# Top-k attention with an MLP behind it: the MLP's input formed in columns from reciprocals that go through HBM, the mean taken out of the weights, and the rows turned back later

## The chip, the cores and the metric

The kernel runs on one core of one Trainium2 chip, one launch. The metric is the device time of that core in microseconds (us). The kernel before took 1569.79 us, the median of three runs (1568.69 to 1570.04).

Engines are named as in the profile: PE (TensorE matmuls; PEld its weight loads), DVE (VectorE), ACT (ScalarE), POOL (GpSimd), SP (SyncE, which here issues DMAs). Each works through its own list of instructions in order and waits for the others at semaphores.

## The reference

Two parts follow each other. The attention has 8 batches, 8 heads, 576 rows and head size 64; each row keeps its 32 largest scores:

```python
scores = scale * np.matmul(q, k.transpose(0, 1, 3, 2))
kth = np.partition(scores, -top_k, axis=-1)[..., -top_k:-top_k + 1]
scores = np.where(scores >= kth, scores, -1000000000.0)
attn = np.exp(scores - np.max(scores, axis=-1, keepdims=True))
attn = attn / (np.sum(attn, axis=-1, keepdims=True) + 1e-09)
attn_out = np.matmul(attn, v)          # (B, H, S, D), then x = (B, S, H*D)
```

Then an MLP with a normalisation in front and a residual, with 512 columns and a hidden width of 2048:

```python
mu = np.mean(x, axis=-1, keepdims=True)
var = np.mean((x - mu) ** 2, axis=-1, keepdims=True)
xn = (x - mu) / np.sqrt(var + 1e-06) * g_ln
return x + np.maximum(xn @ w_ch1, 0.0) @ w_ch2
```

The two weight matrices arrive as 64-bit numbers.

## The kernel before, in words

**Units, groups, blocks.** The attention is cut into 160 *units*: 128 queries of a pair of heads (`hp`, four pairs in a batch), or, for the last 64 queries of a batch, the *rest* of both heads in one unit. One to three units with the same keys are a *group* (80 of them). When all four head pairs of a batch have given the values of 256 queries, these make a *block* of two 128-row tiles for the MLP; the rests of four batches make a block too. There are 18 blocks.

**Steps.** The main loop runs over n. In step n, unit n goes through the search for its 32 largest on DVE (`halve`, then four rounds of `select`), unit n+2 through its scores on PE, unit n-1 through its mask (ACT, then POOL L535) and exponentials (ACT L543, `weigh`, which also gives the row sums `den`), and an older unit is turned, by PE or by DVE and a way through HBM (`move`, `pt<-turned`), so that a group's `values` can be multiplied on PE a *lag* of two to four steps after its last unit. What an engine does in which order is fixed by this program order.

**Filling.** The MLP's matmuls stand in a list, `todo`. Eight times in a step `fill` takes from it as much as a planner gives (`slot` in step n spreads what is left evenly up to the next block that joins, at `give`), unless the first item may not yet run. Ages counted in such ticks also set when late work (`Later`) is issued.

**From values to the MLP, before.** `values` leaves the product for a group in PSUM, transposed: 128 partitions are two heads' 64 columns, the free axis is the queries. `take_values` (L687, ACT) copies it to oT. `place` turns each 128 queries back with a PE transpose (`xo`, L714), and `put` (L691, ACT) copies the two heads' halves to the rows x, each scaled by its row's reciprocal sum, which is a number per partition there. Rests are gathered by POOL (L705) from two batches, and their sums by small DMAs (`keep_den`, L659), for `place_rest` (L721). A step after the last head pair `stats` takes mean and variance on DVE (L742, L743) and the row's mean is taken off x, on DVE for block 0 (L745), on POOL later (L748, L751). Six ticks later `turn_x` turns the rows into xT (PE L778, ACT L781). Then 64 matmuls with w1 (`hidden`, L819), ReLU (L842), and the projection with w2: plainly (L858) for two blocks, by a scheme with seven products instead of eight (L979, with sums on POOL) for the others. `finish` multiplies by rstd and adds the mean (ACT L797), adds x (POOL L790) and stores.

**Weights.** In steps 0 to 20 the 32 pieces of w1 and w2 (128x512 numbers each) are fetched and made into float32: `split` on ACT and POOL (L164 to L169; for w1, the sign is also multiplied by the gain g_ln on POOL, L171), `shift` on DVE (L177), `join` on POOL (L183, L185). A hidden or projection matmul may be issued one step after its piece is `ready`.

Of the kernel before, what the change touches and what calls it, by code (L numbers as in the profile page):

```python
# [29 lines left out]
def compute(  # L30
# [42 lines left out]
    otpool = pool("ot", 1)  # L73
    restpool = pool("ot_rest", 1)
# [3 lines left out]
    xpool = pool("x", 4)  # L78
    rpool = pool("r", 2)
# [3 lines left out]
    xtpool = pool("xt", 1)  # L83
# [29 lines left out]
    columns = const([P, J + NC], "columns")  # L113
    half, gcol = columns[:, 0:J], columns[:, J : J + NC]
    nc.gpsimd.memset(half[:], -0.5)
    w1 = const([P, NC, DFF], "w1")
# [6 lines left out]
    class Piece:  # L123
# [22 lines left out]
        def fetch(self):  # L146
            self.raw = xpool.tile([P, DM, 2], U32, tag="x", name="raw")
            nc.sync.dma_start(self.raw[:].rearrange("p n w -> p (n w)"), self.src)

        def split(self):  # L150
            i = self.i
            high = self.raw[:, :, 1].bitcast(FP32)
            if i < 3 * NC:
                self.size = hpool.tile([P, DM], U32, tag="h", name="size")[:]
                self.low = wt_rows[:, i % 8]
                homes = ((opool, "o"), (opool, "o"), (rpool, "r"), (rpool, "r"), (xtpool, "xT"))
            else:
                self.size = wt_rows[:, 2 * i % 8].bitcast(U32)
                self.low = wt_rows[:, (2 * i + 1) % 8]
                homes = ((opool, "o"), (opool, "o"), (rpool, "r"))  # L160
# [9 lines left out]
            if self.i < NF:  # L170
                nc.gpsimd.tensor_scalar(  # L171
                    self.sign[:], self.sign[:], gcol[:, self.c : self.c + 1], 1.0,
                    ALU.mult, ALU.mult,
                )
# [6 lines left out]
        def join(self):  # L181
# [4 lines left out]
            ready[self.i] = now[0]  # L186
# [3 lines left out]
    ready = [None] * (2 * NF)  # L190
    pieces = [Piece(i) for i in range(2 * NF)]
# [3 lines left out]
    def load_gain():  # L195
        ps = turned()
        nc.tensor.transpose(ps[:, 0:NC], grow[:], ident[0:NC, 0:NC])
        nc.scalar.copy(gcol[:], ps[:, 0:NC])

# [337 lines left out]
    def weigh(u, t):  # L537
# [3 lines left out]
        col = 2 * u.qt + t  # L541
# [5 lines left out]
        if u.rest:  # L547
            den = g.den[:, 2 * J : 2 * J + 1]
        elif u.weighed == 2 and u is [x for x in g.units if not x.rest][-1]:
            whole = [qt for qt in g.qts if qt < J]  # L550
            den = g.den[:, 2 * whole[0] : 2 * whole[-1] + 2]
            g.sums = den
        else:
            return
        nc.scalar.activation(den, den, AF.Copy, bias=DEN_EPS)
# [94 lines left out]
    xs, xps, rs, oTr, dr = {}, {}, {}, {}, {}  # L650

    def keep_den(u):

        b, hp = u.job.b, u.job.hp
        if (b // 2) not in dr:
            dr[b // 2] = denpool.tile([P, H], FP32, tag="dr", name="dr")
        r0 = R * (b % 2)
        for h in range(2):
            nc.sync.dma_start(  # L659
                dr[b // 2][r0 : r0 + R, 2 * hp + h : 2 * hp + h + 1],  # L660
                u.group.den[h * R : (h + 1) * R, 2 * J : 2 * J + 1],
            )
# [21 lines left out]

    def take_values(g):
        g.oT = otpool.tile([P, GQ], FP32, tag="oT", name="oT")
        nc.scalar.copy(g.oT[:, 0 : g.nq], g.av[:, 0 : g.nq])  # L687

    def put(dst, ps, c0, den, d0):
        for h in range(2):  # L690
            nc.scalar.mul(  # L691
                dst[:, c0 + h * D : c0 + (h + 1) * D],
                ps[:, h * D : (h + 1) * D],
                den[:, d0 + h : d0 + h + 1],
            )

    def place(g):

        b, hp = g.job.b, g.job.hp
        for i, qt in enumerate(g.qts):  # L700
            if qt == J:
                if b % 2 == 0:
                    oTr[hp] = restpool.tile([P, P], FP32, tag=f"oTr{hp}", name="oTr")
                r0 = R * (b % 2)
                nc.gpsimd.tensor_copy(  # L705
                    oTr[hp][:, r0 : r0 + R], g.oT[:, i * P : i * P + R]
                )
                continue
            if (b, qt) not in xs:
                pair = xpool.tile([P, 2, DM], FP32, tag="x", name="x")  # L710
                for j in range(2):
                    xs[b, qt // 2 * 2 + j] = pair[:, j]
            ps = brief("xo")
            nc.tensor.transpose(ps[:, 0:P], g.oT[:, i * P : (i + 1) * P], ident[:])  # L714
            put(xs[b, qt], ps, hp * P, g.den, 2 * qt)

    def place_rest(b, hp):
        if hp == 0:
            rs[b // 2] = rpool.tile([P, DM], FP32, tag="r", name="r")[:]
        ps = brief("xo")  # L720
        nc.tensor.transpose(ps[:, 0:P], oTr[hp][:], ident[:])  # L721
        put(rs[b // 2], ps, hp * P, dr[b // 2], 2 * hp)

    class Block:
        def __init__(self, tiles, dsts):
# [4 lines left out]
            self.step = {}  # L732
# [3 lines left out]
        def stats(self, i):  # L736
# [5 lines left out]
            nc.vector.bn_stats(out=st[:], in_=x)  # L742
            nc.vector.bn_aggr(out=self.mv[:, i, :], in_=st[:])  # L743
            if now[0] <= gives_first:
                nc.vector.tensor_scalar_sub(x, x, self.mv[:, i, 0:1])  # L745
            else:
                less = brief_small.tile([P, 1], FP32, tag="less", name="less")
                nc.gpsimd.tensor_scalar(  # L748
                    less[:], self.mv[:, i, 0:1], -1.0, 0.0, ALU.mult, ALU.add
# [727 lines left out]
```

## Time and profile before

| | |
|---|---|
| median of three runs | 1569.79 us (1568.69 to 1570.04) |
| the profiled execution, its time | 1571.11 us |
| the profiled execution, its span | 1569.2 us |
| granted TensorE clock, mean | 0.975 |
| HBM traffic over the span | 155 GB/s |

The span runs from the first to the last instruction on the core; the time holds a little more around it. A row of groups reads: line, engine, operation, out<-in, shapes, count | busy us, mean ns of one | idle time of the engine just before them, and what ended it. A row of waits reads: engine and line that waited <- what it waited for: us in total, times, longest. A row in order of time reads: start us, length us, engine, line, operation, with the idle time before it in brackets. Durations of PE are those of overlapping, modelled instructions. Lines of DMA issues give the median time from issue to landing as their last number.

### The profile page before, as it was taken

Reading aid. Unit: us, or ns where it says so; the run is one execution under the profiler, and the core shown is the slowest. Engines: PE = TensorE matmul, PEld = TensorE weight load, DVE = VectorE, ACT = ScalarE, POOL = GpSimd, SP = SyncE. Lnnn points to the kernel's source line nnn. Section 1 sums busy time; section 2 is a strip of 40 time slices with the busy share of each in tenths; the row PEclk is TensorE's granted clock in tenths of the full one; section 3 lists DMA queues with packets and bytes.
Section 4 is the critical chain, followed back from the end, with each engine's and each line's share of the span. In section 5 each row is a group of like instructions: output and inputs, shape, how many; then the busy total and the mean of one; then the engine's idle time right before and its main releaser. Section 6 shows DMA issues by size and latency. Waiting matters only on the chain. (4 is left out here: it accounts for less than half of the span.)

```text
span 1569.2 us, 27215 instructions
## 1 busy us (share of the span) xinstructions
PE 1469.0 (94%) x8046; PEld 1108.0 (71%) x8046; DVE 1363.4 (87%) x3873; ACT 1083.8 (69%) x3081; POOL 981.2 (63%) x1318
## 2 busy tenths in 40 slices
PE   4568889999999999999999999999999998999997
PEld 3346446566787677778777777777777776788886
DVE  7997999899979998999988999999999999768000
ACT  6978887786777767767768676768676776555421
POOL 6968995747465565756566647474746475737524
PEclk9779989999999999999999999999999999999999
DMA  6623551466728865577754687657677557454511
GB/s 170 167 85 97 137 139 53 124 178 181 226 83 194 202 208 153 168 199 153 216 148 134 174 200 197 173 150 191 175 201 206 162 164 208 121 166 125 150 35 50
DMA packets 374774, 245.60 MB, mean 157 GB/s; under 512 B 255956, under 2 KB 343512, under 8 KB 374616
## 3 DMA queue, kind: packets, MB, share of 16 engines
q1 hardware_dynamic: 371048, 243.17, 57.6%
q8 instruction: 67, 1.10, 0.3%
q10 hardware_dynamic: 3568, 0.59, 0.3%
q14 instruction: 91, 0.75, 0.2%
HBM read 166.14 MB, written 77.53 MB: 155 GB/s over the span
## 5 line engine op out<-in xcount | busy, mean ns | idle before, releaser
L535 POOL TENSOR_TENSOR e<-e,sc 128x576 f32<-128x576 f32 x288 | 416.0, 1462 | 453.8 <-ACT e L532 392.9
L819 PE MATMUL hps<-xT,w 128*128 128x256 f32 x2304 | 542.2, 384 | 2.4 <-ACT xT L781 2.4
L819 PEld LDWEIGHTS hps<-xT,w 128*128 128x128 f32 x2304 | 423.0, 191 | 82.2 <-issue 27.2
L483 DVE MAX8 m<-hi 128x8 f32<-128x296 f32 (+1 forms) x1152 | 471.3, 444 | 1.2
L469 DVE MATCH_REPLACE8 hi<-m,hi 128x288 f32<-128x288 f32 (+1 forms) x864 | 377.0, 441 | 0.0
L979 PE MATMUL ops<-w,h 128*128 128x256 f32 x1280 | 304.8, 383 | 1.4 <-ACT o L944 1.4
L979 PEld LDWEIGHTS ops<-w,h 128*128 128x128 f32 x1280 | 233.6, 190 | 44.3 <-issue 13.5
L419 ACT COPY sc<-scps 128x288 f32<-128x288 f32 x576 | 188.5, 402 | 78.5 <-POOL e L535 56.2
L543 ACT ACTIVATE e<-e,m 128x576 f32<-128x576 f32 x288 | 225.1, 784 | 14.6 <-POOL e L535 12.5
L532 ACT ACTIVATE e<-sc,m 128x576 f32<-128x576 f32 x288 | 209.4, 769 | 0.0
L842 ACT ACTIVATE h<-hps 128x512 f32<-128x512 f32 x144 | 86.7, 602 | 114.1 <-PE hps L819 113.5
L577 DVE STREAM_TRANSPOSE sc<-e 128x1152 f32<-128x1152 f32 x87 | 118.8, 1366 | 52.5 <-ACT e L543 46.3
L669 PE MATMUL av<-pt,vb 128*64 128x256 f32 (+2 forms) x1280 | 148.8, 376 | 9.5 <-DMA pt<-turned 7.7
L462 DVE TENSOR_TENSOR lo<-sc 128x576 f32<-128x576 f32 (+1 forms) x160 | 136.1, 850 | 0.0
L461 DVE TENSOR_TENSOR hi<-sc 128x576 f32<-128x576 f32 (+1 forms) x160 | 130.0, 812 | 3.0 <-ACT sc L419 3.0
L669 PEld LDWEIGHTS av<-pt,vb 128*64 128x64 f32 x1280 | 81.6, 140 | 66.4 <-issue 17.1
L438 PE MATMUL scps<-kT,late_qT 64*128 64x288 f32 (+3 forms) x832 | 121.7, 410 | 0.2 <-ACT pt L618 0.2
L979 PE MATMUL ops<-wt,s 128*128 128x256 f32 x512 | 119.4, 383 | 0.0
L475 DVE MAX8 hi<-lo 128x8 f32<-128x288 f32 x288 | 117.5, 443 | 0.0
L438 PE MATMUL scps<-kT,qT 64*128 64x288 f32 x512 | 92.6, 460 | 23.5 <-DVE qT L366 8.0
L606 PE MATMUL tp<-ident,e 128*128 128x128 f32 x456 | 74.2, 290 | 39.9 <-ACT e L543 28.9
L979 PEld LDWEIGHTS ops<-wt,s 128*128 128x128 f32 x512 | 94.7, 190 | 17.3 <-issue 4.4
(111 smaller groups left out, 1793.5 us busy)
## 6 DMA issues: line engine op xcount, KB each, us to landing
turned<-sc SPq DMA_DIRECT2D x87, 576.0 KB, 4.2
pt<-turned SPq DMA_DIRECT2D x348, 144.0 KB, 3.2
w<-forms SPq DMA_DIRECT2D x128, 256.0 KB, 4.7
vb<-in_v_dram SPq DMA_DIRECT2D x80, 288.0 KB, 4.2
raw<-in_moe_w_ch_dram SPq DMA_DIRECT2D x32, 512.0 KB, 4.5
kT<-kept SPq DMA_DIRECT2D x48, 288.0 KB, 3.7
kept<-kT SPq DMA_DIRECT2D x32, 288.0 KB, 3.6
kqin<-in_k_dram SPq DMA_DIRECT2D x116, 72.0 KB, 2.6
```

The source lines that it names most:

```text
L419: nc.scalar.copy(u.sc[:, t, s * HALF : (s + 1) * HALF], u.made[s][t][:, 0:HALF])
L438: nc.tensor.matmul(ps[i * R : i * R + ql, o : o + width], qT[r, q0 : q0 + ql], kT[r, k0 : k0 + width], start=True, stop=True,)
L461: nc.vector.tensor_tensor(hi, a, b, ALU.max)
L462: nc.vector.tensor_tensor(lo, a, b, ALU.min)
L469: nc.vector.match_replace(x, m[:, t, :], x, LOWEST)
L483: nc.vector.max(m[:, t, :], u.hi[:, t, r0 : r0 + width])
L532: nc.scalar.activation(u.e[:, t], u.sc[:, t], AF.Relu, bias=u.edge[:, t : t + 1], scale=-STEEP)
L535: nc.gpsimd.tensor_tensor(u.e[:, t], u.e[:, t], u.sc[:, t], ALU.subtract)
L543: nc.scalar.activation(u.e[:, t], u.e[:, t], AF.Exp, bias=u.bias[:, t : t + 1], scale=-scale, accum_out=g.den[:, col : col + 1],)
L669: nc.tensor.matmul(av[h * D : (h + 1) * D, 0 : g.nq], vb[:, h * (J + 1) + c, :], heads_of(g, h, 0, g.nq // 32)[:, :, c], start=(c == 0), s ...
L819: nc.tensor.matmul(ps[0][:, side * N : (side + 1) * N], w1[:, c, f * P : (f + 1) * P], self.xT[:, c, 0:N], start=(c == 0), stop=(c == NC - 1),
L979: nc.tensor.matmul(bank[name][:, 0:Q], a(j), rhs, start=first and j == 0, stop=(j == G - 1), skip_group_check=not first,)
```

## The change

What the MLP takes is now formed without turning the values first. `take_values` copies the product straight into its place in xT (or rTs for rests). The reciprocals of a group's sums are taken in one DVE instruction, sent to HBM number by number (`keep_shares`), and read back spread over the 64 partitions of each head (`fetch_shares`); POOL multiplies xT by them in place (`place`). The mean is taken out of the weights: with W the gain-scaled w1, (x - mean(x)) @ W = x @ (W - column means of W), so a PE product with a matrix that holds -g/512 gives the column means on all partitions (`means`), and one DVE instruction for each of the 16 pieces forms W*g + mean in place (`centre`); the product with g on POOL goes. A piece of w1 is `ready` after that. The hidden matmuls start on xT at once; after the first 24 of them `turn_x` turns xT back to rows x, for statistics and the residual. `finish` no longer adds the mean.

The pools move too: x has three buffers for a row tile each, xT three, the rests' xT two, the shares one; the raw weights lie in those of xT. Before the second tile of a block is turned, `close` issues what is still waiting of the block before.

```diff
             nc.scalar.activation(self.sign[:], high, AF.Sign)
-            if self.i < NF:
-                nc.gpsimd.tensor_scalar(
-                    self.sign[:], self.sign[:], gcol[:, self.c : self.c + 1], 1.0,
-                    ALU.mult, ALU.mult,
-                )
...
+    def means(n):
+        nb = centred_parts[0]
+        if nb * NC >= NF or not all(map(done, joined[nb * NC : (nb + 1) * NC])):
+            return None
+        centred_parts[0] += 1
+        ps = product("mean")
+        for c in range(NC):
+            nc.tensor.matmul(
+                ps[:], gmean[:, c * P : (c + 1) * P], pieces[nb * NC + c].dst,
+                start=(c == 0), stop=(c == NC - 1),
+            )
+        return nb, ps
+
+    def centre(made, cs):
+        nb, ps = made
+        for c in cs:
+            x = pieces[nb * NC + c]
+            nc.vector.scalar_tensor_tensor(
+                x.dst, x.dst, gcol[:, c : c + 1], ps[:], ALU.mult, ALU.add
+            )
+            ready[x.i] = now[0]
...
+    def keep_shares(g):
+        nc.vector.reciprocal(g.sums, g.sums)
+        kept = g.kept = hbmpool.tile([2 * J + 1, P], FP32, tag="shares", name="shares")
+        n = g.sums.shape[1]
+        sends.add(lambda: nc.sync.dma_start(kept[0:n].rearrange("c p -> p c"), g.sums))
+
+    def fetch_shares(g):
+        t = g.shares = sharepool.tile([P, GQ], FP32, tag="shares", name="shares")
+        n = sum(qt < J for qt in g.qts)
         for h in range(2):
-            nc.sync.dma_start(
-                dr[b // 2][r0 : r0 + R, 2 * hp + h : 2 * hp + h + 1],
-                u.group.den[h * R : (h + 1) * R, 2 * J : 2 * J + 1],
-            )
+            rows = slice(h * D, (h + 1) * D)
+            if n:
+                nc.sync.dma_start(
+                    t[rows, 0 : n * P].rearrange("d (j p) -> d j p", p=P),
+                    g.kept[h : 2 * n : 2].unsqueeze(0).to_broadcast([D, n, P]),
+                )
...
     def take_values(g):
-        g.oT = otpool.tile([P, GQ], FP32, tag="oT", name="oT")
-        nc.scalar.copy(g.oT[:, 0 : g.nq], g.av[:, 0 : g.nq])
-
-    def put(dst, ps, c0, den, d0):
-        for h in range(2):
-            nc.scalar.mul(
-                dst[:, c0 + h * D : c0 + (h + 1) * D],
-                ps[:, h * D : (h + 1) * D],
-                den[:, d0 + h : d0 + h + 1],
-            )
+        for to, cols in home_of(g):
+            nc.scalar.copy(to, g.av[:, cols])

     def place(g):
...
-            ps = brief("xo")
-            nc.tensor.transpose(ps[:, 0:P], g.oT[:, i * P : (i + 1) * P], ident[:])
-            put(xs[b, qt], ps, hp * P, g.den, 2 * qt)
...
+        for to, cols in home_of(g):
+            nc.gpsimd.tensor_tensor(to, to, g.shares[:, cols], ALU.mult)
...
     def turn_x(self, i):
...
+            number = blocks.index(self)
+            if number and i == 1:
+                close(blocks[number - 1])
             tp = turned()
             for c in range(NC):
                 nc.tensor.transpose(
-                    tp[:, c * P : (c + 1) * P], self.x[i][:, c * P : (c + 1) * P], ident[:]
+                    tp[:, c * P : (c + 1) * P], self.xT[:, c, i * P : (i + 1) * P], ident[:]
                 )
+            x = self.x[i] = xpool.tile([P, DM], FP32, tag="x", name="x")
+            nc.scalar.copy(x[:], tp[:])
+            rows_of.setdefault(now[0] + 1, []).append((self, i))
...
     def give(n):
...
         for blk in gives[n]:
             rows, hidden, project = blk.items()
...
+            todo.extend(hidden[:ROWS_AT] + rows + hidden[ROWS_AT:] + project)
...
+        if g:
+            fetch_shares(g)
         if quick:
             values(g)
             take_values(g)
...
+        averaged, fresh_means = fresh_means, means(n)
...
+        for x in recips.pop(n, []):
+            keep_shares(x)
         if nxt:
             halve(nxt)
```

More of the change, by code (lines that the diff above doesn't have):

```diff
@@ L546, in weigh @@
         )
[L547 to L555, printed above, removed]
+        if u is g.units[-1] and u.weighed == len(u.tiles):
+            n = 2 * len(g.qts) - u.rest
+            g.sums = g.den[:, 0:n]
+            nc.scalar.activation(g.sums, g.sums, AF.Copy, bias=DEN_EPS)
     def heads_of(g, h, i0, i1):
@@ L717, in place_rest, with home_of @@
[L717 to L722, printed above, removed]
+    def home_of(g):
+        b, hp = g.job.b, g.job.hp
+        whole = [qt for qt in g.qts if qt < J]
+        homes = []
+        if whole:
+            key = b, whole[0]
+            if key not in xTs:
+                xTs[key] = xtpool.tile([P, NC, 2 * P], FP32, tag="xT", name="xT")
+            homes.append((xTs[key][:, hp, 0 : len(whole) * P], slice(0, len(whole) * P)))
+        if J in g.qts:
+            key = b // 4
+            if key not in rTs:
+                rTs[key] = restpool.tile([P, NC, 2 * P], FP32, tag="rest", name="rest_xT")
+            r0, n = b % 4 * R, len(whole) * P
+            homes.append((rTs[key][:, hp, r0 : r0 + R], slice(n, n + R)))
+        return homes
@@ L731, in __init__ @@
             self.mv = None
-            self.step = {}
             self.ready = False
```

175 lines of the change are left out of this document (68 added, 107 removed).

## The prediction

> **What bounds the kernel now.** I read the page's shares and slices first, then cut the run into stretches by what is full, then asked each stretch who waits. Part 1 and two of the slice rows of the page:
>
> ```profile
> PE 1469.0 (94%) x8046; PEld 1108.0 (71%) x8046; DVE 1363.4 (87%) x3873; ACT 1083.8 (69%) x3081; POOL 981.2 (63%) x1318
> ...
> PE   4568889999999999999999999999999998999997
> ...
> DVE  7997999899979998999988999999999999768000
> ```
>
> No share names the limit: PE is short of work in the first six slices (some 240 us), where DVE is full; then both are full; in the last five PE alone. The stretches, with busy time per engine (columns: length, PE, PEld, DVE, ACT, POOL, clock, DMA share, GB/s):
>
> ```profile
> 0.00:242.30 242.30, 173.38 (x795) 109.83 (x796) 216.74 (x584) 199.33 (x516) 198.55 (x190) 0.87 0.50 132
> 242.30:1308.20 1065.90, 1048.62 (x5997) 793.15 (x5996) 1029.04 (x2975) 776.89 (x2284) 646.86 (x916) 1.00 0.64 171
> 1308.20:1317.90 9.70, 6.16 (x44) 4.11 (x42) 9.63 (x27) 6.58 (x20) 5.82 (x9) 1.00 0.81 226
> 1317.90:1467.00 149.10, 148.71 (x762) 122.34 (x763) 104.13 (x280) 78.69 (x212) 85.59 (x124) 1.00 0.57 157
> 1467.00:1569.20 102.20, 92.17 (x454) 78.60 (x452) 3.87 (x12) 22.30 (x52) 44.39 (x84) 0.97 0.18 54
> ```
>
> A, to 242 us: PE lacks 69 us of work, DVE 26; DVE sets the pace, POOL and ACT (199 each) close behind. B, to 1308: PE lacks 17.3 of 1065.9, DVE 36.9; PE is the longer by 19.6 us, with little room under it. C, the rest: PE alone, but for a hole of 3.5 us around 1313 and ten us, mostly of POOL and stores, in which PE has ended.
>
> **The change, part by part.**
>
> *The transposes of the values go.* Each of the 80 groups turned its oT back with two `xo` transposes, the rests with 16 more. What one is worth on PE is read from starts in the order of time, not from the mean duration, since matmuls overlap:
>
> ```profile
> 1009.15 2.86 PE L819 MATMUL hps<-xT,w 128*128 128x256 f32 x12
> 1011.84 0.38 PE L714 MATMUL xo<-ident,oT 128*128 128x128 f32 x2
> 1012.06 2.76 PE L819 MATMUL hps<-xT,w 128*128 128x256 f32 x12
> ...
> L714 PE MATMUL xo<-ident,oT x128: 272/273/476, 57.0 to 1496.5; 128*128 128x128 f32 x128
> L721 PE MATMUL xo<-ident,oTr x16: 272/273/273, 623.4 to 1309.0; 128*128 128x128 f32 x16
> ```
>
> Two take 1012.06 - 1011.84 = 0.22 us, so 0.11 each (and a 128x256 matmul 2.69 / 12 = 0.22). Nine groups have their values in A (18 transposes), eight after B (16), so B loses 128 - 34 + 16 = 110: 12.1 us; C loses 1.8; in A they are free. The 144 transposes `tp<-ident,x` stay in number; they now turn xT into rows. B can gain between 0 (DVE binds after all) and 12.1. PE was longer by 19.6, more than is taken, so I take four fifths: -9.7.
>
> *288 scaled copies `put` leave ACT* (first row below; 32 more for the rests), 36 row copies take the place of 36 xT copies, 16 small copies come. ACT is 73% busy in B and bounds nothing there: 0, under PE's matmuls; without that cover it would be a gain. Four products that lay out the mean's weights (128x128, near L691's 0.31: 1.2 us) come on ACT before the first weights are split, and lie under POOL's saving on the same pieces (L171, below): 0.
>
> *Centring moves from rows to weights.* On PE 16 `mean` matmuls of 128x512 come, all in steps 3 to 13 of A, where PE lacks 69 us; at the 0.641 of the last row below they are 10.3 us and hidden. On DVE 16 `centre` instructions come (one 128x512 tile in SBUF, a column, and the mean in PSUM), four each in steps 4, 6, 10 and 14, all in A where DVE is the bound; two subtractions L745 go.
>
> ```profile
> L691 ACT ACTIVATE x<-xo,den 128x64 f32<-128x64 f32 x256 | 58.6, 311 | 17.2 <-DVE den L1350 9.5 <-PE xo L714 7.5
> L742 DVE BATCH_NORM_STATS2 st<-x 128x6 f32<-128x512 f32 x32 | 21.5, 673 | 38.2 <-ACT x L691 38.2
> L745 DVE TENSOR_SCALAR x<-x,mv 128x512 f32<-128x512 f32 x2 | 1.0, 487 | 0.1
> L462 DVE TENSOR_TENSOR lo<-sc 128x576 f32<-128x576 f32 x11 | 13.1, 1191 | 0.0
> L858 PE MATMUL ops<-w,h 128*128 128x512 f32 x128 | 65.4, 641 | 0.3 <-POOL w L185 0.3
> ```
>
> Ends: 0.487 (L745) and 1.191 (L462, two tiles in SBUF, between 120 and 240 us): 7.8 to 19.1 us. I take L742's 0.673, one 128x512 tile read once: +10.8, less 1.0 for L745. Why L462 is so far from it shows in the spread of its twin against an instruction with one input (min/median/max):
>
> ```profile
> L461 DVE TENSOR_TENSOR hi<-sc x160: 429/737/1978, 11.3 to 1440.8; 128x576 f32<-128x576 f32 x128, 128x288 f32<-128x288 f32 x32
> L483 DVE MAX8 m<-hi x1152: 414/443/471, 12.7 to 1449.9; 128x8 f32<-128x288 f32 x96, 128x8 f32<-128x296 f32 x96
> ```
>
> L461 stretches to 1978, MAX8 never beyond 471. The Trainium skill ("SBUF — State Buffer", section "SBUF: two separate sides") says that GpSimd and VectorE share one port pair as an exclusive lock, and that a VectorE operation needs it in a two-port mode or with two SBUF inputs. By that rule a centre, whose second tile is in PSUM, is not held up and the sum stays at +10.8; were it held up as L462 is, the term would be 19.1. The two rows agree with the rule; no row of before has that mix of inputs.
>
> What A gets back are DVE's waits (waited for, us in total, times, longest), in A:
>
> ```profile
> DVE wt L177 <- POOL wt L165: 9.3, 6, 3.4
> DVE size L177 <- POOL size L165: 3.6, 5, 1.3
> DVE st L742 <- ACT x L691: 2.7, 1, 2.7
> ...
> 108.62 0.58 ACT L781 COPY xT<-tp 128x512 f32<-128x512 f32 x1 [1.87 <-PE tp L778]
> 110.36 0.59 ACT L781 COPY xT<-tp 128x512 f32<-128x512 f32 x1 [1.15 <-PE tp L778]
> ...
> L171 POOL TENSOR_SCALAR sign<-sign,columns 128x512 f32<-128x512 f32 x16 | 17.0, 1065 | 3.4 <-ACT sign L169 1.6 <-ACT m L495 0.8
> ```
>
> The statistics of block 0 move from step 9 to step 12, behind rows that were turned in step 11: -2.7. The 9.3 us of steps 10 and 11 are late weights: POOL waited for ACT, and ACT stood in the turning of block 0 (1.87 + 0.58 + 1.15 + 0.59 = 4.2 us), which now comes 24 hidden matmuls later: -4, between 0 and -9.3. The 16 products of sign and gain L171 leave POOL, of 3.6 us of waits for it I take -1. The weights w1 are ready two steps later, so steps 13 and 14 issue three and none of their hidden matmuls, made good by step 17 under 69 us of idle PE: 0, and +1.3 if step 15 becomes PE's. A in all: 10.8 - 1.0 - 2.7 - 4 - 1 = +2.1, between -5 and +15.
>
> *POOL.* 64 products of 128x256 and 32 of 128x64 (`place`) come; L171, the centring (L751, L748) and the rests' copies (L705) go:
>
> ```profile
> L963 POOL TENSOR_TENSOR o<-o,t 128x256 f32<-128x256 f32 x32 | 25.3, 792 | 14.0 <-ACT t L953 14.0
> L751 POOL TENSOR_SCALAR x<-x,less 128x512 f32<-128x512 f32 x30 | 24.8, 826 | 3.1
> L751 POOL TENSOR_SCALAR r<-r,less 128x512 f32<-128x512 f32 x4 | 3.8, 945 | 0.4
> L748 POOL TENSOR_SCALAR less<-mv 128x1 f32<-128x1 f32 x34 | 8.3, 245 | 23.2 <-DVE mv L743 23.1
> L705 POOL COPY oTr<-oT 128x64 f32<-128x64 f32 x32 | 7.5, 236 | 11.3 <-ACT oT L687 9.2 <-DVE hi L469 1.8
> ```
>
> 64 x 0.792 + 32 x 0.3 (near L705's 0.236) = 60 us against 17.0 + 24.8 + 3.8 + 8.3 + 7.5 = 61. POOL's load stays, idle time of 39% in B covers it: 0. A place that waits holds the masks L535 of the next step behind it, and so ACT's exponentials.
>
> *DMAs on SP.* 80 sends of the reciprocals (512 or fewer single numbers each) and 192 fetches that spread them over 64 partitions come; 64 `dr<-den` go: 208 more. Nearest landings:
>
> ```profile
> pt<-turned SPq DMA_DIRECT2D x348, 144.0 KB, 3.2
> dr<-den SPq DMA_DIRECT2D x64, 0.2 KB, 2.8
> ...
> L659 SPq DMA_DIRECT2D dr<-den x64: 461/588/1463, 427.7 to 1287.6; - x64
> ...
> PE av L669 <- DMA pt<-turned: 6.3, 5, 2.9
> DVE st L742 <- ACT x L691: 15.3, 4, 4.9
> ```
>
> A send and a fetch are 2.8 + 3.2 = 6.0 us in sequence. The reciprocal is DVE's last but one work of a step, ahead of the next unit's two L461/L462. The fetch opens the next step (lag 3, 16 groups of B) or the one after (lag 4), and the place is in that step's middle. A step of B is 1065.9 / 127 = 8.4 us, so at lag 3 the place comes about 2 x 0.74 + 4 = 5.5 us after the reciprocal and POOL waits half a microsecond; at lag 4 not at all. On SP the fetch waits for the send's landing, and the send for DVE's reciprocal; queued behind are the pt loads of a group's last unit. PE waited for pt 6.3 us in B; I take half as much again, +3, between 0 and +19 (half of one issue on SP, 0.588, reaching PE at each of B's 63 groups). The last row is DVE's wait for rows in B; rows now come from a turn instead of a put, also one step ahead: 0. So B is -9.7 + 3 = -6.7.
>
> *C.* In step 148 the planner had nothing to issue (rows of the next block not centred); now it issues 25 matmuls for 8:
>
> ```profile
> 1311.92 1.95 PE L669 MATMUL av<-pt,vb 128*64 128x256 f32 x16 [1.44 <-DMA pt<-turned]
> 1316.21 1.06 PE L778 MATMUL tp<-ident,x 128*128 128x128 f32 x8 [1.91 <-ACT sc L419]
> ...
> L790 POOL TENSOR_TENSOR o<-o,x 128x512 f32<-128x512 f32 x32 | 41.4, 1304 | 21.2 <-ACT o L797 21.2
> ```
>
> 17 x 0.22 = 3.7 us of work for a hole of 3.5, of which 1.44 is a DMA's: -2.5, between 0 and -3.5. Transposes -1.8. New: there are three row buffers, so the copy of a block's second rows on ACT takes that of the previous block's first rows and waits until POOL has added them to the output (L790, last row), with ReLU copies queued behind it and PE behind those. In the three dense blocks I take 0.5 each, +1.5, between 0 and 3 x 1.3 = 3.9; in B the steps between are twice as long: 0. C: -2.8.
>
> Sum: 2.1 - 6.7 - 2.8 = -7.4 us. The profiled execution took 1571.1, 1.3 above the median of 1569.8, so 1563.7 there and 1562.4 as median; a change of 0.2% (3.1 us) is about what can be told from none.
>
> **Rivals.**
>
> 1. *More of it* (for: DVE's waits in A sum to 15.6 and PE is the longer in B; against: both engines are full side by side). A at -5, B at -12.1 + 1, C at -4: 1550.
> 2. *DVE is the second bound in B, and the transposes buy nothing* (for: 1029.0 of 1065.9; against: PE's 19.6 us more). 2.1 + 0 + 0 - 2.8 with no new DMA wait: 1569, the same.
> 3. *Slower: the centres cost what L462 costs, and nothing is absorbed* (place: steps 4, 6, 10, 14; for: DVE's slices in A are nearly full; against: none of L462's second SBUF input). A at 19.1 - 1.0 = +18, the rest as forecast: 1578. It decides once A grows by more than 9.5 us.
> 4. *Slower: the way through HBM delays the pt loads or the places* (for: SP executes in order; against: most groups have a whole step to spare). 63 x 0.3 = 19 in B in place of 3: 1578; it decides from (3 + 7.4) / 63 = 0.17 us for a group.
>
> **How the numbers follow.** Forecast 0.46 (its own range 1556 to 1567), more 0.12, the same 0.14, centres 0.13, HBM 0.15. The first two are faster, of the third a quarter either side: faster 0.61, same 0.08, slower 0.31. The range 1549 to 1582 holds the cases but for the ends of 1 and 4.
>
> **What would show it.** Right: no `xo` on PE; A longer by about 2 us, with centres near 0.67 and the L177 waits halved; B shorter by 7, PE's waits for pt under 10 us; no hole after 1300. Wrong: centres above 1 us, PE waiting in B for ACT or for the xT products, POOL `place` waiting for DMAs over 2 us, or B unchanged with DVE without gaps.

## The result, and the profile after

The changed kernel takes 1822.66 us in the median of four runs (1814.75 to 1830.22) against 1569.91 (1568.69 to 1570.32): a ratio of 1.161, 95% interval 1.156 to 1.167. The forecast was 1562.4, the range 1549 to 1582. The profiled execution took 1830.2 with a span of 1828.1 us. The stretches of the prediction, each cut here some 4 us later in its step than there (columns as there: length, PE, PEld, DVE, ACT, POOL, clock, DMA share, GB/s):

```profile
0.00:274.95 274.95, 187.88 (x835) 118.48 (x836) 230.87 (x608) 196.71 (x489) 182.10 (x179) 0.86 0.43 118
274.95:1564.00 1289.05, 1098.16 (x5870) 816.42 (x5869) 1055.04 (x2975) 729.30 (x2057) 680.66 (x915) 0.92 0.68 148
1564.00:1828.10 264.10, 246.44 (x1233) 204.09 (x1231) 117.45 (x307) 100.37 (x252) 135.36 (x207) 0.98 0.48 122
```

A is longer by 32.7 us, B by 223, C by 3; counted from the start of the same units on DVE (`halve` of units 21 and 148) it is 29, 222 and 7. In B no engine is full any more (PE 85%, DVE 82% of the stretch), and DMAs lead the waits. Who waits, over the whole run of the changed kernel (us in total, times, longest):

```profile
POOL xT L738 <- DMA shares<-shares: 175.6, 24, 11.1
DVE sc L597 <- ACT e L568: 155.8, 36, 11.9
...
PE av L699 <- DMA pt<-turned: 80.2, 13, 10.4
...
POOL rest_xT L738 <- DMA shares<-shares: 71.6, 10, 14.9
```

Its own view of SP's queue (L607 brings a unit's pt, L682 and L687 fetch the shares):

```profile
SPq L607 <- DMA turned<-sc: 223.4, 55, 10.1
SPq L682 <- DMA shares<-den: 186.4, 30, 10.0
...
SPq L687 <- DMA shares<-den: 92.2, 14, 8.5
```

And its DMA issues (count, KB each, median us from issue to landing), below them two rows of the kernel before:

```profile
turned<-sc SPq DMA_DIRECT2D x87, 576.0 KB, 7.1
pt<-turned SPq DMA_DIRECT2D x348, 144.0 KB, 3.0
kT<-kept SPq DMA_DIRECT2D x48, 288.0 KB, 5.7
shares<-shares SPq DMA_DIRECT2D x128, 64.0 KB, 4.0
...
shares<-den SPq DMA_DIRECT2D x48, 2.0 KB, 9.8
shares<-den SPq DMA_DIRECT2D x16, 0.5 KB, 7.8
shares<-den SPq DMA_DIRECT2D x16, 2.5 KB, 9.3
```

```profile
turned<-sc SPq DMA_DIRECT2D x87, 576.0 KB, 4.2
...
kT<-kept SPq DMA_DIRECT2D x48, 288.0 KB, 3.7
```

The smallest transfers are the slowest shown. A send of half a KB lands in 7.8 us, one of two KB in 9.8, where the prediction had 2.8. And the large transfers, which the change does not touch, land later as well: turned<-sc at 7.1 in place of 4.2. From there the waits run on. SP stands before L607 and L682, pt is late for PE, the shares are late for POOL's product, behind which POOL's masks and ACT's exponentials queue, and DVE's L597 waits for those.

Three theories could tell this story. **Q**: SP works in order and stands in its list until a send has landed, so all that is queued behind is late. **S**: the writes of single 4-byte numbers into HBM hold up the transfers themselves. **R** is that the rest of the change (centres, products on POOL, rows turned later) is what costs.

### The profile page after: what moved, and what is told of

The parts are those of the page before. It is cut to its first block, busy times and chain, and to the rows that moved or that the text cites. A ratio compares the mean times of both kernels' runs of the same rounds, so it can differ in the third digit from the quotient of the medians.

```text
span 1828.1 us, 26987 instructions
## 1 busy us (share of the span) xinstructions
PE 1532.5 (84%) x7934; PEld 1139.0 (62%) x7934; DVE 1403.4 (77%) x3887; ACT 1026.4 (56%) x2797; POOL 998.1 (55%) x1299
## 5 line engine op out<-in xcount | busy, mean ns | idle before, releaser
L814 PE MATMUL hps<-xT,w 128*128 128x256 f32 x2048 | 493.6, 392 | 6.6 <-POOL xT L738 4.3
L814 PEld LDWEIGHTS hps<-xT,w 128*128 128x128 f32 x2048 | 387.0, 195 | 85.4 <-issue 26.4
L975 PEld LDWEIGHTS ops<-w,h 128*128 128x128 f32 x1280 | 243.3, 196 | 71.2 <-issue 17.4
L699 PE MATMUL av<-pt,vb 128*64 128x256 f32 (+2 forms) x1280 | 174.0, 422 | 123.0 <-DMA pt<-turned 80.2
L597 DVE STREAM_TRANSPOSE sc<-e 128x1152 f32<-128x1152 f32 x87 | 119.3, 1371 | 187.3 <-ACT e L568 155.8
L738 POOL TENSOR_TENSOR xT<-xT,shares 128x256 f32<-128x256 f32 x64 | 48.6, 760 | 350.2 <-DMA shares<-shares 175.6
L699 PEld LDWEIGHTS av<-pt,vb 128*64 128x64 f32 x1280 | 92.8, 157 | 191.9 <-issue 148.8
L487 DVE TENSOR_TENSOR lo<-sc 128x576 f32<-128x576 f32 (+1 forms) x160 | 152.8, 955 | 0.0
L463 PE MATMUL scps<-kT,qT 64*128 64x288 f32 x512 | 98.9, 467 | 47.5 <-ACT x L782 11.8
L486 DVE TENSOR_TENSOR hi<-sc 128x576 f32<-128x576 f32 (+1 forms) x160 | 136.1, 851 | 3.0 <-ACT sc L444 3.0
L463 PEld LDWEIGHTS scps<-kT,late_qT 64*128 64x128 f32 (+1 forms) x832 | 72.3, 170 | 76.5 <-issue 29.4
```

What stands on the lines that cost most here:

```text
L463: nc.tensor.matmul(ps[i * R : i * R + ql, o : o + width], qT[r, q0 : q0 + ql], kT[r, k0 : k0 + width], start=True, stop=True,)
L486: nc.vector.tensor_tensor(hi, a, b, ALU.max)
L487: nc.vector.tensor_tensor(lo, a, b, ALU.min)
L699: nc.tensor.matmul(av[h * D : (h + 1) * D, 0 : g.nq], vb[:, h * (J + 1) + c, :], heads_of(g, h, 0, g.nq // 32)[:, :, c], start=(c == 0), s ...
L814: nc.tensor.matmul(ps[0][:, side * N : (side + 1) * N], w1[:, c, f * P : (f + 1) * P], self.xT[:, c, 0:N], start=(c == 0), stop=(c == NC - 1),
L975: nc.tensor.matmul(bank[name][:, 0:Q], a(j), rhs, start=first and j == 0, stop=(j == G - 1), skip_group_check=not first,)
```

## The experiments

Unless an interval is given, each is one run, beside the kernel before on the same chip (1568.59 to 1571.62 us, one run or the median of several).

**SP's standing, or the sends.** In the first run no fetch depends on its own group's send any more: all groups fetch the first group's numbers.

```diff
+        first_kept.append(g.kept)
+        kept = first_kept[0]
...
-                    g.kept[h : 2 * n : 2].unsqueeze(0).to_broadcast([D, n, P]),
+                    kept[h : 2 * n : 2].unsqueeze(0).to_broadcast([D, n, P]),
```

> The changed kernel, but every group fetches the reciprocals of the first group, which have long been in HBM; all 80 sends stay. The output is wrong by that. Theory Q (SP stands in its list until a group's send has landed, 9.1 us in the middle of the sends, and the loads behind it come late): 1580 us (1555 to 1620), SP's waits for shares<-den nearly gone, PE's waits for pt<-turned back under 15 us. Theory S (the sends' single numbers themselves clog the DMA engines, whoever waits): above 1740. Theory R (the rest of the change costs the time): above 1740.

1843.71 us: no better. Before the fetches SP now waited 23 us for a send's landing, where it had waited 279, and POOL waited for the fetches as before, though their data had lain in HBM since the first group (waits of this kernel):

```profile
POOL xT L743 <- DMA shares<-shares: 205.3, 28, 13.3
```

In the second the fetch stays and moves behind its send, just ahead of the product:

```diff
-        if g:
-            fetch_shares(g)
...
         if g and not quick:
+            fetch_shares(g)
             place(g)
```

> The changed kernel, with the fetch issued just ahead of the products that need it instead of at the start of the step, so that in SP's list the pt loads, the key loads and the stores of that step stand ahead of it; output as the reference. Theory Q: a large part comes back, 1640 to 1760, with POOL still waiting for the shares. Theories S and R: 1800 or more.

1892.24 us: worse, with POOL's wait for the shares at 422.1 us. Q falls with these two as the main cause: taking away most of SP's standing for the sends gave nothing back.

**The form of the send.** The third run sends the same bytes, each partition's numbers side by side, so that a send of 2 KB is 128 pieces of 16 bytes.

```diff
-        sends.add(lambda: nc.sync.dma_start(kept[0:n].rearrange("c p -> p c"), g.sums))
+        sends.add(lambda: nc.sync.dma_start(
+            kept[0:n].rearrange("c p -> (c p)").rearrange("(p c) -> p c", c=n), g.sums))
```

> The changed kernel, but a send writes each partition's numbers side by side (128 pieces of 8 to 20 bytes instead of 128 to 640 single numbers); the fetch reads the same bytes after waiting for it, so the numbers arrive in another order and the output is wrong. If the length of a send is in its single numbers, it lands in 2.5 to 4 us instead of 9.1. Theory Q: SP waits a few us less for each group, 1590 to 1680. Theory S: the same range or lower, 1570 to 1650. Theory R: above 1780.

1621.56 us: four fifths of the loss are gone with the single numbers. Its DMA issues:

```profile
turned<-sc SPq DMA_DIRECT2D x87, 576.0 KB, 4.8
...
shares<-den SPq DMA_DIRECT2D x48, 2.0 KB, 3.8
shares<-den SPq DMA_DIRECT2D x16, 0.5 KB, 8.3
shares<-den SPq DMA_DIRECT2D x16, 2.5 KB, 2.7
```

The pieces of 16 and 20 bytes land in 3.8 and 2.7 us. The 16 lone rests have one number for each partition and are still sent as 128 single numbers; they still take 8.3.

**The trip on its own.** To the kernel before, only the reciprocals, sends and fetches are added (the fetches into HBM); nothing uses them.

```diff
+        inv = g.den[:, 2 * J + 1 : 2 * J + 1 + n]
...
+            nc.vector.reciprocal(inv[:, 0:w], g.den[:, n0 : n0 + w])
...
+        kept = g.kept = hbmpool.tile([2 * J + 1, P], FP32, tag="shares", name="shares")
+        sends.add(lambda: nc.sync.dma_start(kept[0:n].rearrange("c p -> p c"), inv))
...
+        if g:
+            fetch_shares(g)
```

> The kernel before, with nothing of the change but the way through HBM: at the end of the same steps a reciprocal of each group's sums into spare columns and the same send, and at the start of the same steps the same fetches (into HBM, there being no room on the chip), whose result nothing reads. Theory Q: the round trip alone makes it slow, 1740 to 1840. Theory S: the same. Theory R: 1570 to 1600.

1923.41 us. Then the sends alone, with the fetches taken out again:

> The kernel before, with the reciprocals a second time and the sends of single 4-byte numbers into HBM added; nothing fetches them (the output is the reference's). S: 1750 to 1930 us, most of what the kernel before with send and fetch lost (1923.41): the writes alone hold up the others. If it takes the fetches (or SP's standing before them): 1570 to 1620 us.

1796.09 us: 80 writes of 2.5 KB or less, which nothing reads, cost the kernel before 224 us. R falls as the main cause. What makes the fetches into HBM cost another 127 us there (1923.41 against 1796.09) was not taken apart. The waits of this kernel, PE's and then SP's queue:

```profile
PE av L682 <- DMA pt<-turned: 74.6, 11, 9.4
```

```profile
SPq L587 <- DMA turned<-sc: 366.5, 64, 11.6
```

**Whether the number of pieces or where they land counts.** Three runs change only the places in HBM that the same single numbers are written to, and one sends them into SBUF. With w = 4, 16 and 128 elements for each number they lie 16, 64 and 512 bytes apart:

```diff
-        kept = g.kept = hbmpool.tile([2 * J + 1, P], FP32, tag="shares", name="shares")
-        sends.add(lambda: nc.sync.dma_start(kept[0:n].rearrange("c p -> p c"), inv))
+        kept = g.kept = hbmpool.tile([(2 * J + 1) * P, w], FP32, tag="shares", name="shares")
+        sends.add(lambda: nc.sync.dma_start(
+            kept[0 : n * P, 0:1].rearrange("(c p) o -> p (c o)", p=P), inv))
```

> The kernel before plus the sends alone (1796.09 us with the numbers side by side in HBM), the same 4-byte numbers now written 512 bytes apart, so that no two share a stretch of HBM. N (neighbouring numbers from different partitions meet in HBM and wait for each other): under 1640 us, landing below 5 us. K (each small write to HBM costs by itself): 1750 to 1830 us, landing 7 to 12 us as before.

> The kernel before plus the sends alone, the 4-byte numbers written 16 bytes apart in HBM (side by side: 1796.09 us, landing about 8 to 9; 512 bytes apart: 1577.88 us, landing 2.5 to 3.2). W (numbers wait for the others that fall into the same short stretch of HBM, one after another): in between, landing 3.5 to 5 us, as the 16-byte pieces sent side by side had (3.8), and 1580 to 1660 us. A (only numbers that touch each other hinder each other): as at 512 bytes, landing under 3.3 and 1575 to 1582 us. If it takes a stretch of 512 bytes alone: landing 7 to 10, near 1796.

> The same with the numbers 64 bytes apart. W: as at 512 bytes, landing under 3.3 us and 1575 to 1585 us, if the stretch is 64 bytes or shorter; A: the same. If the stretch is longer than 64 bytes (512): landing 3.5 to 8 us and 1590 to 1750 us.

The run into SBUF (with one buffer less for the sums):

```diff
-        kept = g.kept = hbmpool.tile([2 * J + 1, P], FP32, tag="shares", name="shares")
-        sends.add(lambda: nc.sync.dma_start(kept[0:n].rearrange("c p -> p c"), inv))
+        kept = g.kept = sumpool.tile([P, J + 1, 2], FP32, tag="shares", name="shares")
+        sends.add(lambda: nc.sync.dma_start(kept[:, 0:n, 0], inv))
```

> The kernel before plus the same sends as single 4-byte numbers, written into an SBUF tile, 8 bytes apart within each partition, instead of HBM; nothing reads them. If it is the number of pieces (128 to 640 a send): 1750 to 1830 us, as with HBM. If it is HBM as their destination: 1569 to 1600 us, landing 2.5 to 4 us as the kernel before's sums had (2.8). My bet is HBM.

| the same single numbers | us |
|---|---|
| HBM, side by side | 1796.09 |
| HBM, 16 bytes apart | 1588.94 |
| HBM, 64 bytes apart | 1576.83 |
| HBM, 512 bytes apart | 1577.88 |
| SBUF | 1579.86 |

The DMA issues with 16 bytes between numbers, then 64, then into SBUF:

```profile
turned<-sc SPq DMA_DIRECT2D x87, 576.0 KB, 4.8
...
shares<-den SPq DMA_DIRECT2D x48, 2.0 KB, 3.9
shares<-den SPq DMA_DIRECT2D x16, 0.5 KB, 3.1
```

```profile
shares<-den SPq DMA_DIRECT2D x48, 2.0 KB, 3.2
shares<-den SPq DMA_DIRECT2D x16, 0.5 KB, 3.1
```

```profile
shares<-den SPq DMA_DIRECT2D x48, 2.0 KB, 3.2
shares<-den SPq DMA_DIRECT2D x16, 0.5 KB, 2.9
```

The number of pieces is the same in all five rows, so it is not what costs. What costs is that numbers written as single pieces fall close together in HBM: 16 numbers within 64 bytes are dear, four cost 12 us more than one, and from 64 bytes on nothing more is gained. In all these runs the neighbours came from different partitions; whether that matters is not shown. The distance fits the third run, where a partition's 16 bytes are one piece. It does not contradict a landing that does not grow with the size of a send (7.8 us for 128 numbers, 9.3 for 640). My bet on HBM against SBUF was half right, since HBM is as quick when the numbers lie apart. Which part of the chip makes neighbours wait is not shown. The Trainium skill ("DMA: Bandwidth & Descriptors", section "Specifications") has transfers below 512 bytes done as read-modify-write; it names no effect of the distance between such writes, and here 4-byte writes 64 bytes apart cost 6 us in all, side by side 224.

**What the change is worth without the dear sends.** Only the first group sends, and all fetch its numbers:

```diff
-        sends.add(lambda: nc.sync.dma_start(kept[0:n].rearrange("c p -> p c"), g.sums))
+        if not first_kept:
+            sends.add(lambda: nc.sync.dma_start(kept[0:n].rearrange("c p -> p c"), g.sums))
```

> The changed kernel, in which only the first group sends its numbers to HBM and all groups fetch these (so every other group's values are multiplied by the first group's numbers, and the output is not the reference's); reciprocals, fetches, products and the rest of the change stay. It measures what the change is worth without its 63 other sends. S (the single 4-byte numbers written into HBM hold up the other transfers): 1555 to 1575 us, since only my other terms are left (their sum put the kernel at 1562.4, of which 3.0 was the way through HBM). R (the rest of the change costs the 53 us that the kernel with numbers sent side by side still had): about 1620 us.

1572.08 us. From the first run (1843.71 us) this kernel differs in the sends alone (79 of the 80 are gone, not 63), so these cost 272 us, and S explains the loss but for a few us. The rest of the change gains nothing over the whole, where my sum without the trip gives 1559.4. But the one send that is left is still of single numbers side by side, and in A SP stands until it has landed, as Q has it: the fetch behind it starts at 58.88 us, and the next load of weights at 61.28, where the kernel below that turns its numbers on DVE has 53.38 and 55.79. POOL then waits 11.0 us for the fetch, ACT 8.3 for the weights, and DVE for ACT's sums (the send, then POOL's and DVE's waits up to 245 and 244.5 us):

```profile
shares<-den SPq DMA_DIRECT2D x1, 2.0 KB, 8.2
```

```profile
POOL xT L744 <- DMA shares<-shares: 13.6, 2, 11.0
DVE den L671 <- ACT den L575: 11.6, 2, 7.2
```

A is 248.5 us here, 6.2 more than before, and 243.5 in that other kernel. So some 5 of the 1572 us are that first send's, an estimate from these two lengths: the rest of the change would then be worth some 4 us.

**Sends that work.** The first turns the numbers on PE and sends rows of 512 bytes, the second does so half a step earlier:

```diff
-        sends.add(lambda: nc.sync.dma_start(kept[0:n].rearrange("c p -> p c"), g.sums))
+        ps = brief("turned_sums")
+        nc.tensor.transpose(ps[0:n, 0:P], g.sums, ident[:])
+        row = sharepool.tile([P, GQ], FP32, tag="shares", name="row")[:, 0:P]
+        nc.scalar.copy(row[0:n], ps[0:n, 0:P])
+        sends.add(lambda: nc.sync.dma_start(kept[0:n], row[0:n]))
```

> The changed kernel, whose numbers are turned on PE into rows of 128 before they are sent (one transpose of 128 x n and one ACT copy a group, 64 groups), so that a send is 1 to 5 rows of 512 bytes in place of 128 to 640 single numbers; it computes the reference. S: 1560 to 1590 us: what the send of single numbers cost is gone for the 1-number rests too, +0.4 us a group on PE and ACT at most (64 x 0.4 = 26 us if none of it is covered). R: about 1620 us as with the numbers sent side by side. If what counts is the number of pieces of the fetches, 1620 us as well, with SP still waiting some 100 us for the numbers.

> The kernel with turned rows, and the reciprocal behind the first selection of its step in place of the step's end, transpose, copy and send behind the products of that step (from step EARLY on; the reference is computed). S: 1555 to 1580 us, 0 to 15 us below the kernel with turned rows, since the send leaves half a step (4 us) sooner and SP no longer stands before the fetch. If SP's waits for the numbers cost nothing, the two agree within 3 us.

1599.78 and 1578.82 us. The difference fits a wait that I had not expected, PE's for a reciprocal at the end of DVE's list, which falls to 1.5 us in the second (waits in B of the first of the two):

```profile
PE turned_sums L675 <- DVE den L671: 25.7, 16, 4.8
```

In the second DVE, whose reciprocal now stands ahead in its list, waits 39.1 us in B for the sums instead (14 times). The third turns them on DVE in blocks of 32 x 32, and sends rows of 128 bytes (with one buffer for the rows, and two in place of four for the sums):

```diff
+        nc.vector.reciprocal(wide[:, 0:n], g.sums)
+        row = sumpool.tile([P, 32], FP32, tag="row", name="row")
+        nc.vector.transpose(row[:], wide[:])
...
+            for i in range(P // 32):
+                nc.sync.dma_start(kept[0:n, i * 32 : (i + 1) * 32], row[i * 32 : i * 32 + n])
```

> The changed kernel, whose numbers are turned on DVE in blocks of 32 x 32 (one transpose of 128 x 32 a group, 80 groups) and sent as 4 to 20 rows of 128 bytes in four transfers; reciprocal and transpose stand behind the first selection of a step as in the kernel turned early; nothing added on PE or ACT. The reference is computed. S (only single numbers were dear): 1565 to 1580 us, as with one send (1572.08), and 0 to 12 us under the kernel turned early on PE (1578.82), whose 80 transposes PE no longer makes. If rows of 128 bytes are still small enough to hold the others up: over 1590 us, with turned<-sc landing above 5 us.

1581.65 us, ratio 1.0062 (1.0045 to 1.0079): the change with a cheap send, still slower than before, and not better than the turn on PE. Its stretch A is 243.5 us, B 1083.4, C 253.9. In B, DVE waits for the sums and for the buffer that a send still holds:

```profile
DVE wide L675 <- ACT den L578: 26.5, 11, 5.1
DVE row L677 <- DMA shares<-row: 8.0, 3, 6.8
```

Against B of the kernel with one send (1066.7 us) DVE is busy 7.8 us more (1039.65 against 1031.82) and idle 8.9 us more. So the sends are cheap here, but not the way to them: in the kernels with the earlier reciprocal DVE stands before sums that ACT has not yet made. Rows of 128 bytes with the reciprocal left at the step's end were not tried.

**Where the saved PE work went.** In B of the kernel with one send PE's longest stalls are rows' turns that wait for a bank of PSUM (7.7 us in two). The next two runs give these turns a bank of the products:

```diff
-            tp = turned()
+            tp = product("tp")
```

> The kernel with numbers turned on DVE (1581.65 us), whose rows' turns (four transposes and an ACT copy) take a PSUM bank from the products' three instead of the five that scores and transposes share; the order of instructions is the same on every engine and the reference is computed. G (the 13.8 us of PE work that the change takes out of stretch B came back as PE's stalls for a bank that ACT empties late, 15 us with the scores, and as the lower clock behind each stall): 1560 to 1573 us, no rows' turn waiting for the scores' copies, and the granted clock of B back near 1.00. H (those stalls only move to the products, which find two banks taken): 1577 to 1590 us.

> The same move of the rows' turns to the products' banks in the kernel with one send (1572.08 us), where the trip costs nothing. G: 1555 to 1566 us, that is what I had forecast for the change without its trip (1559.4). H: 1570 to 1580 us.

1576.92 us (ratio 1.0038, 1.0024 to 1.0051) and 1571.74 us. Moving the banks moved the stalls: at step 52 the products now wait where the rows had waited. With the turn on DVE it gave 4.7 us back, just outside H, where G asked for 9 or more; with one send it gave nothing.

Perhaps DVE hid the saving, being busy over 99% in 900 to 1300 us of both kernels. The next two runs leave out one round of the selection in each kernel:

```diff
-        if i < TOP_K // 8 - 1:
+        if i < TOP_K // 8 - 2:
```

> The kernel before without the third round of match_replace (two tiles of 0.55 us a step, so the 32nd largest score is taken as the 24th and the output is not the reference's). It makes DVE's list some 1 us a step shorter in both kernels, so that PE sets the pace where DVE did. Expected: 1480 to 1555 us, more the more of the kernel is paced by DVE; its stretch B is the measure for the next run.

> The same round left out of the changed kernel with one send (1572.08 us against 1571.62 for before). D (where DVE is busy over 99% of the time, as in 900 to 1300 us of both kernels, the PE work that the change takes out is hidden behind it): with DVE's list shorter the saving appears, B is 9 to 16 us shorter than that of the kernel before without the round, and the total 5 to 18 us below. H (PE's stalls behind ACT and the DMAs, and the clock after them, eat it whatever DVE does): B within 4 us of each other.

1547.41 and 1550.17 us. B of the kernel before without the round, and PE's longest wait in it:

```profile
240.80:1286.30 1045.50, 1041.72 (x5991) 790.39 (x5992) 959.20 (x2530) 780.52 (x2286) 681.41 (x916) 1.00 0.65 175
```

```profile
PE hps L819 <- ACT xT L781: 2.2, 1, 2.2
```

B of the kernel with one send, without the round, and PE's waits:

```profile
246.20:1292.30 1046.10, 1033.81 (x5877) 783.30 (x5876) 958.57 (x2537) 733.07 (x2066) 681.12 (x915) 1.00 0.65 182
```

```profile
PE tp L784 <- ACT sc L444: 3.6, 2, 2.0
PE av L705 <- DMA kept<-kT: 2.9, 1, 2.9
PE av L705 <- DMA late_qT<-kept: 2.2, 2, 1.4
PE av L705 <- DMA pt<-turned: 1.6, 2, 1.2
```

With DVE at 959 of 1046 in both, B is the same length. PE is busy 7.9 us less and idle 8.5 us more (12.3 against 3.8). D falls, H stands, on one run each: stalls behind ACT's copies and the loads take what the transposes gave. The totals are 2.8 us apart; the second kernel's A is 5.4 us the longer (246.2 us against 240.8), and there too its one send lands in 8.2 us.

The last run leaves the fetches out too, so that the way through HBM is used once:

```diff
+        if first_kept:
+            g.shares = first_shares[0]
+            return
```

> The changed kernel with one send and now one fetch as well: all groups multiply by the first group's numbers, which stay in SBUF, so the output is not the reference's; the way through HBM is gone but for its first use. L (the fetches, 10 MB over 80 groups on SP, make the loads that PE waits for come late: kT<-kept, kept<-kT, pt<-turned): 1556 to 1566 us, PE's waits for DMAs in B under 4 us. M (the loads and the ACT copies are late for the shorter PE by themselves): 1569 to 1575 us, as with the fetches (1572.08).

1566.59 us, ratio 0.9977 (0.9967 to 0.9987), just outside L's 1566. PE's waits in B:

```profile
PE tp L790 <- ACT sc L444: 7.6, 2, 4.7
PE scps L463 <- ACT sc L444: 4.7, 3, 2.7
...
PE av L709 <- DMA kT<-kept: 0.7, 1, 0.7
```

PE waits 0.7 us in B for a load. The fetches, 9 MB on SP, are what made the loads late; that is worth some 5 us. The stalls behind ACT are left, and B (1060.0 us) gains 5.9 of the 9.7 us forecast without the trip. A is 250.0 us, with the first group's send landing in 8.6 us; with the 243.5 us of the kernel that turns on DVE in its place, the total would be some 1560 us, an estimate close to the 1559.4 of the sum. No kernel that sends and fetches all its numbers was faster than the one before.

## Why the prediction was wrong

**The step that failed** is "A send and a fetch are 2.8 + 3.2 = 6.0 us in sequence", with "+3, between 0 and +19" for B behind it, where PE's waits for pt were to grow from 6.3 to some 9 us and grew to 77. The fetch was nearly right (4.0 after, 3.2 with one send). The send was priced by `dr<-den`, single numbers into SBUF. The run into SBUF shows that this price holds there, for 640 numbers too (landing 2.1 to 3.2 us). Into HBM side by side it was 7.8 to 9.8. The second half of the error is that I priced the send only by who waits for it. It costs 224 us with nobody waiting, since it delays the other transfers (`turned<-sc` from 4.2 to 7.1 us in the changed kernel). My bounds were taken from a transfer with another destination, and the upper one (0.3 us a group) said nothing of interference.

Point by point:

- *Rival 4* had the place (pt late, places waiting), with the chance 0.15, and a price of 0.3 us a group; measured it was 222 / 63 = 3.5 in B. Its mechanism, SP in order, was not the main cause.
- *The centres* took what was forecast (one line of the changed kernel; min/median/max):

```profile
L220 DVE SCALAR_TENSOR_TENSOR w<-w,columns,mean x16: 699/733/740, 56.3 to 190.9; 128x512 f32<-128x512 f32 x16
```

  16 x 0.733 = 11.7 us against 10.8. None stretched, so rival 3 falls, and the rule of the Trainium skill ("SBUF — State Buffer", section "SBUF: two separate sides") agrees for an instruction whose second tile is in PSUM.
- *A at +2.1*: +1.2 with the numbers turned on DVE, +1.9 with the early turn on PE, so right where the first send is cheap too; with that send of single numbers left in, A was +6.2 with one send and +7.7 with one trip. The waits of L177 nearly went, by more than the 5 us that I took for them and the gain product: from 12.9 us to 0.7 in the kernel that turns on DVE, whose waits of DVE in A are

```profile
DVE wide L675 <- ACT den L578: 6.2, 2, 4.4
...
DVE size L176 <- POOL size L169: 0.5, 1, 0.5
DVE wt L176 <- POOL wt L169: 0.2, 1, 0.2
```

  What took their place is that DVE waits for the sums of the first groups, a new wait that the prediction did not name.
- *B at -9.7 without the trip*: -5.9 with one trip, +0.8 with the fetches, +17.5 with all sends cheap on DVE (-4.8, +1.9 and +18.6 counted from the start of the same units on DVE). The 110 transposes went as counted (two for each of 64 groups, not of 80); in the pair with the shorter list PE's busy time fell by 7.9 of their 12.1 us. The rest fits the clock, which was 0.97 in 600 to 700 us and 0.98 in 1100 to 1200 of the second kernel of the pair and 1.00 in the same stretches of the first: up to 3 + 2 = 5 us, an estimate. Taking four fifths of the 12.1 as time was the mistake: "PE was longer by 19.6, more than is taken" asks only which of two engines is fuller. PE then stalled for ACT's copies, and for loads that the fetches made late. That the copies had been just in time for a longer PE is likely, but no run shows it.
- *POOL at 0*: its product took 0.760 us (forecast 0.792), and POOL stayed under cover in the kernels with cheap sends.
- *C at -2.8*: -6 to -8 in the kernel that turns on DVE and those with one send or one trip (252.7 to 254.9 us against 261.0). PE did not wait in C of the first of them, where it had waited 4.2 us before; the direction was right, the size was under half. The row copies that wait for POOL's addition took 3.1 us in four times, where I had 1.5.
- *Rival 2*, that the transposes buy nothing, came near the outcome of the one-send kernel (1572.08 against its 1569), but by other terms (A +6.2, B +0.8, C -6.1), and not for its reason: with a shorter list for DVE they bought nothing either.
- *A count*: 16 of the sends hold 640 numbers, not "512 or fewer". It changes no sum.

## What to carry to other kernels

Do not write single numbers from many partitions side by side into HBM: turn them on chip first, into rows of 128 bytes or more, or leave 64 bytes between them (tried only with nothing that reads them); 80 such writes of 2.5 KB or less, side by side, cost 224 us. Price a transfer by a row with the same destination and the same piece size, and ask also what it does to the transfers beside it, not only who waits for it. Work taken from the fullest engine need not come back as time: ask for each of its waits how late the other side already is. And when a run leaves out a dear step for all groups but one, look at what that one still costs.

## What the hardware showed that was not expected

Beside the distance in HBM, the granted clock: a short stall of PE costs more than its length. Around a stall of 2.99 us that ends at 1175.6, in B of the kernel with one send (columns as above):

```profile
1170.00:1175.00 5.00, 2.62 (x16) 1.51 (x15) 4.96 (x19) 4.94 (x13) 1.78 (x3) 0.99 0.62 181
1175.00:1180.00 5.00, 4.39 (x13) 3.68 (x14) 4.90 (x13) 3.06 (x8) 5.00 (x5) 0.50 0.42 139
1180.00:1185.00 5.00, 5.00 (x27) 3.65 (x27) 5.00 (x16) 2.47 (x8) 4.27 (x8) 0.83 0.89 256
1185.00:1190.00 5.00, 5.00 (x32) 3.35 (x29) 4.93 (x15) 1.19 (x4) 2.15 (x5) 1.00 0.53 99
```

In the five us after the stall the clock is 0.50, in the next five 0.83, and PE works for 4.39 of the first and all of the second, so it loses up to another 0.5 x 4.39 + 0.17 x 5 = 3.0 us, as much as the stall itself. The Trainium skill ("TensorE: Matmul & The Clock Gate", section "What's actually happening") says that the clock halves after an idle window of some 3.4 us and comes back after a busy one; the 0.50 agrees, and here a stall under 3 us was enough. Over 250 to 1300 us the clock was 0.93 in one stretch of 50 us and 0.97, 0.98, 0.97 and 0.97 in four of 100 with one send, and 0.97 in one of 50 and 0.98 in one of 100 before: up to 14.5 us against 3.5, an estimate, so the lower clock may have taken most of what the transposes gave there.
